# A kernel for attention and two mixtures of experts: the sum and the sending of an expert's second tile stand behind the branch over its third tile

## The chip, the cores and the metric

One core of one Trainium2 chip. The metric is the time of one execution on the device in microseconds (us), and of several runs the median.

## The reference

Three layers follow one another on 4608 tokens of 512 numbers, in float32:

```python
attn = exp(scale * q_c @ k_c^T - max) / (sum + 1e-9); x = attn @ v_c   # in chunks of 64, 8 heads
# _moe_ref
do_compute = x @ w_skip > 0
logits = xc @ w_gate; e_idx = argmax(logits); gate_w = softmax(logits)[e_idx]
for e in range(8):                          # each token that is computed goes to one expert
    h = maximum(xc[mask] @ w1[e], 0)        # 512 -> 1024
    y[mask] = gate_w[mask, None] * (h @ w2[e])
out = x.copy(); out[do_compute] = xc + y    # the other tokens stay as they are
# _moe2_ref
h = maximum(maximum(x @ w1, x @ w2), x @ w3)
return h @ w_out
```

How many tokens an expert gets is known only when the kernel runs.

## The kernel before, in words

The core does the attention (up to some 175 us), the middle layer of eight experts (some 190 to 480 us) and the last layer (to the end). Every number is held as a high and a low part, so a product of two matrices is three products on TensorE (PE): `mm3`, lines 663 to 665.

**Tokens.** The attention leaves its rows in `x_dram`. For each expert the rows of its tokens are gathered in tiles of 128 by indirect DMAs of GpSimd (POOL) (`gather`, L554 to L564), through a list of slots. A tile's result is added to its rows by VectorE (DVE) and sent back by an indirect DMA of POOL (`put_back`, L940 to L949: the sum is L941, the send L943). Two buffers of four tiles hold rows; expert e uses buffer e mod 2, named `xg_4030` for experts 2, 4 and 6 and `xg_4126` for 1, 3, 5 and 7 in what follows. So tile j of expert e + 2 may be gathered only when tile j of expert e has been sent; `gather_tiles` says so by a dependency on that send. Sends and gathers go out in POOL's program order, and each waits for the one that used its semaphore (`DMASW0` to `DMASW7`, in turn) before it.

**One expert.** For experts 1 to 6 `first_tiles` computes the first two tiles together:

- `h`: 96 products of 256 columns, which ScalarE (ACT) and DVE evacuate as `hhi` and `hlo`;
- `ahead`: the next expert's tiles 2 and 3 are gathered, and the rows of this expert's third tile are turned (`trm`, L584, transposes on PE; ACT and DVE evacuate them as `xhi` and `xlo`, L587 and L588);
- `y_0`: the first tile's 24 products and its `put_back`; `amid`, which is `turn_next`, turns the next expert's first two tiles, `trm_0` and `trm_1`;
- `y_1`: the second tile's 24 products and its `put_back`.

Behind that stands the branch `tc.If(n_e[e] > 2 * P)` (L1240): the third tile (`single`) and, inside it, a branch for the fourth (`beyond`, L1189) and for more (L1193, L1194). With this input experts 2, 3 and 5 take the branch, 2 and 3 with a fourth tile; experts 1, 4 and 6 jump over it. Expert 7 begins with one tile alone (`main`), then two more.

**Weights.** An expert has eight pieces of weights. SyncE loads each, ACT makes its high part (`whi`, L93) and DVE its low part (`wlo`, L94). The next expert's pieces 0, 1, 2, 3 and 7 (`EARLY`) are written in front of `first_tiles`, and 6, 4 and 5 (`LATE`) behind the branch. Products of `y` go by `KF_ORDER`, so they use the pieces 7, 6, 4 and 5, six products each.

**Order.** A scheduler sets the order on each engine within a straight stretch of the program, by dependencies and by its own costs. What is bound to a branch can't leave its side of it. Eight banks of PSUM hold accumulators: five "mm", two "tr" for transposes and one "t3"; before the change transposes rotate over all three of `t3, tr, tr`, and `y` over "mm".

Of the kernel before, what the change touches and what calls it, by code (L numbers as in the profile page):

```python
# [40 lines left out]
def kernel(  # L41
# [15 lines left out]
    nc = tc.nc  # L57
# [12 lines left out]
    def ps(tag, name):  # L70
        pool, bufs = banks[tag]
        return pool.tile([P, 512], F32, tag=tag, name=name, bufs=bufs)
# [4 lines left out]
    def take_turns(**tags):  # L77
        for use, among in tags.items():
            turns[use] = cycle(among)

    def ps_mm(name):
        return ps(next(turns["mm"]), name)
# [466 lines left out]
    def apart(ins, own, other):  # L549
        for grp in (own, other):  # L550
            tc.declare_no_dep(ins.ins, group=grp, reason="tiles of tokens share no row")
        tc.add_to_no_dep_group(own, ins.ins)
# [98 lines left out]
    vm, big, big_T, units, xt, groups, slots, picks, xgs, xT, link, put, sent = {}, {}, {}, {}, {}, {}, {}, {}, {}, {}, {}, {}, ([], [])  # L651
# [286 lines left out]


    def put_back(key, xg, ids, acc):  # L940
        nc.vector.scalar_tensor_tensor(  # L941
            xg[:, :DM], acc, xg[:, DM:DM + 1], xg[:, :DM], op0=ALU.mult, op1=ALU.add)
        ins = nc.gpsimd.indirect_dma_start(  # L943
            out=x_dram[:, :], out_offset=bass.IndirectOffsetOnAxis(ap=ids, axis=0),
            in_=xg, in_offset=None,
            bounds_check=N - 1, oob_is_err=False,
        )
        apart(ins, "put", "get")
        put.setdefault(key, []).append(ins.ins.name)  # L949

    def relu_split(hi, lo, src):
        return (
            nc.scalar.activation(hi, src, AF.Relu),
            nc.vector.scalar_tensor_tensor(lo, src, 0.0, hi.bitcast(F32), op0=ALU.max, op1=ALU.subtract),
        )

    def second_acc(name, key, hhi, hlo, i, xg, tag=None):
        n = xg.shape[0]
        acc = (ps(tag, f"y_{name}") if tag else ps_mm(f"y_{name}"))[:n]
        sl = slice(i * P, i * P + n)  # L960
        for n, kf in enumerate(KF_ORDER):
            bhi, blo = ew[key[0], 4 + kf // 2]
            mm3(acc, hhi[:, kf, sl], hlo[:, kf, sl], bhi[:, kf % 2, :], blo[:, kf % 2, :], n == 0, n == 7)
        return acc

    def second(name, key, hhi, hlo, i, xg, ids):
        put_back(key, xg, ids, second_acc(name, key, hhi, hlo, i, xg))

    def first_tiles(name, e, xT, xgs, idss, between, side=(), amid=None):
        hi, lo = xT  # L970
        w = hi.shape[2]
        hhi = bpool.tile([P, 8, w], F32R, tag="b8", name=f"hhi_{name}")
        hlo = bpool.tile([P, 8, w], F32R, tag="b8", name=f"hlo_{name}")
        per = 512 // w
        for n in range(0, 8, per):
            f0 = KF_ORDER[n]
            acc = ps_mm(f"h_{name}_{n}")[:, :per * w].rearrange("p (f t) -> p f t", f=per)
            for j in range(per):
                f = f0 + j
                for c in range(KC):  # L980
                    ahi, alo = ew[e, c]
                    link["main"] = mm3(acc[:, j, :], ahi[:, f * P:(f + 1) * P], alo[:, f * P:(f + 1) * P],
                        hi[:, c, :], lo[:, c, :], c == 0, c == KC - 1)
            done = relu_split(hhi[:, f0:f0 + per, :], hlo[:, f0:f0 + per, :], acc)
            if n % 2 == 2 - per and side:
                with tc.issue_after(done[0].ins), tc.issue_after(done[1].ins):
                    side.pop(0)()
        between()
        for i in range(2):
            second(f"{name}_{i}", (e, i), hhi, hlo, i, xgs[i], idss[i])  # L990
            if i == 0 and amid:
                amid()
        return hhi, hlo

    def single_rows(name):
        return [four_kb([P, 8, P], F32R, f"h{nm}_{name}", True) for nm in ("hi", "lo")]
# [31 lines left out]

    def idc(e, j):
        return ids_0[:, j:j + 1] if e == 0 and j < 3 else ids_sb[:, e * COLS + j:e * COLS + j + 1]  # L1030

    def tiles_of(rows):
        return [rows[:, j, :] for j in range(4)]
# [153 lines left out]
    def beyond(e, t3):  # L1187
        xg = xgs[e][3]
        with tc.If(n_e[e] > 3 * P):  # L1189
            if t3 is None:  # L1190
                t3 = rows_T(f"{e}_3", [xg])
            single(f"{e}_3", (e, 3), t3, xg, idc(e, 3))
            with tc.If(n_e[e] > 4 * P):  # L1193
                with tc.For_i(4, nt_e[e], 1) as j:  # L1194
                    ids = mpool.tile([P, 1], I32, tag="ids", name=f"ids_{e}")
                    nc.vector.tensor_copy(ids, ids_sb[:, bass.ds(j + e * COLS, 1)])
                    gather(xg, ids, alone=True)
                    single(f"{e}_n", (e, 3), rows_T(f"{e}_n", [xg], t3), xg, ids)

    for e in range(E):  # L1200
        def ahead():
            if e + 1 < E:
                gather_tiles(e + 1, [2, 3])
            turn_ahead()

        def turn_ahead():
            xT[e, 2] = rows_T(f"{e}_2", xgs[e][2:3])

        def turn_next():
            if e + 2 < E:  # L1210
                xT[e + 1] = rows_T(f"{e + 1}", xgs[e + 1][:2])
            else:
                xT[e + 1] = rows_T(f"{E - 1}_0", xgs[e + 1][:1])

        if 0 < e < E - 1:
            gather_tiles(e + 1, [0, 1])
        free = [wpool] * ((WA - 2 * held) // 2) + [wpool2] * ((WB - 2 * (E - held)) // 2)
        early_a = len([p for p in free if p is wpool])
        if 0 < e < E - 1:
            for i in EARLY:  # L1220
                expert_piece(e + 1, i, free.pop(0))
        side = [lambda i=i: sums_ahead(i) for i in range(sum(STEPS[:e]), sum(STEPS[:e + 1]))]
        later, side = (side, []) if e == 0 else ([], side)
        if 0 < e < E - 1:
            first_tiles(f"{e}", e, xT[e], xgs[e], [idc(e, 0), idc(e, 1)], ahead, side, turn_next)
        raws = {i: load_raw(*expert_src(e + 1, i)) for i in LATE} if e + 1 < E else {}
        if e == 0:
            n_e, nt_e = [
                [nc.values_load(cnt_i[0:1, c:c + 1], min_val=0, max_val=m) for c in range(c0, c0 + E)]
                for c0, m in ((0, N), (E, COLS))]  # L1230
            n_seam = nc.values_load(cnt_i[0:1, 2 * E:], min_val=0, max_val=N)
        third = (xT[e, 2], xgs[e][2], idc(e, 2)) if e < E - 1 else None
        with ExitStack() as pinned:
            if e == 0:
                for ins in link["rows"]:
                    pinned.enter_context(tc.issue_after(ins.ins))
                for chunk in later:
                    chunk()
            elif e + 1 < E:
                with tc.If(n_e[e] > 2 * P):  # L1240
                    t3 = single(f"{e}_2", (e, 2), *third, lambda: rows_T(f"{e}_3", xgs[e][3:]))
                    beyond(e, t3)
            else:
                main = single(
                    f"{e}_0", (e, 0), xT[e], xgs[e][0], idc(e, 0), lambda: rows_T(f"{e}", xgs[e][1:3]))
                with tc.If(n_seam > 3 * P):
                    for j in (1, 2):
                        single(f"{e}_{j}x", (e, j), rows_T(f"{e}_{j}x", [xgs[e][j]]), xgs[e][j], idc(e, j))
                    beyond(e, None)
                    for j in (1, 2):  # L1250
                        nc.gpsimd.memset(idc(e, j), N)
                load_first()
                sums_room(0, 0)

                def turn_first():
                    with tc.issue_after(link["main"].ins):
                        sums_T(0, 0)

                first_tiles(f"{e}", e, main, xgs[e][1:3], [idc(e, 1), idc(e, 2)], turn_first, side)
                ring_ahead(0, 0, 5)  # L1260
                sums_room(0, 1)
                sums_T(0, 1)
            for n, i in enumerate(LATE if e + 1 < E else []):
                pool = wpool if n < held else wpool2
                early_a += pool is wpool
                expert_piece(e + 1, i, pool, None, raws[i])
        if e == 0:
            beyond(0, None)
        held = early_a
# [65 lines left out]
    for b, (r0, n) in enumerate(BLOCKS):  # L1335
# [31 lines left out]
        for half in range(2):  # L1367
            for i in range(n // P):
                acc = ps_mm(f"o_{b}_{half}_{i}")
# [45 lines left out]
```

## Time and profile before

| | us |
|---|---|
| median of three runs | 1044.71 |
| the three runs | 1044.71, 1053.66, 1044.31 |
| the profiled execution | 1041.12 |
| its span (first to last instruction) | 1039.4 |

The trace is of that one profiled execution; its times count from the start of the span. Each engine has its own row of instructions, so the time that an engine waits in front of an instruction, and what ended that wait, stand in brackets behind the row. A releaser is inferred: where an instruction waits for several things, the one is named that came last by the record, which may not be the one that held it. The record of an indirect DMA on POOL is the instruction; when its data has arrived is told in a row of its own.

### The profile page before, as it was taken

What the parts mean: (1) busy time and instruction counts of PE and PEld (TensorE: products, weight loads), DVE (VectorE), ACT (ScalarE), POOL (GpSimd) and SP (SyncE); (2) the same over time, 40 slices, a digit from 0 to 9 for tenths busy, and PEclk for the clock granted to TensorE, in tenths of its full rate; (3) what the DMA queues carried; (4) which work ended last, traced back from release to release, by engine and by line L of the source; (5) the groups of instructions that cost most, each with busy time, mean ns of one, the idle gap of its engine ahead of it and who ended that gap; (6) DMA issues with size and microseconds to landing.
All of it is one profiled execution on the core that took longest, in us unless ns stands there. A gap on an engine that the chain in (4) does not pass through costs nothing.

```text
span 1039.4 us, 19677 instructions
## 1 busy us (share of the span) xinstructions
PE 993.9 (96%) x7569; PEld 850.8 (82%) x7569; DVE 572.1 (55%) x1100; ACT 420.1 (40%) x762; POOL 316.6 (30%) x359
## 2 busy tenths in 40 slices
PE   7989899998999999899999999999999999999996
PEld 6988898887787898687878888788788888878995
DVE  4667798687282895555897524343334424434241
ACT  5877674455252554333443422223222322223230
POOL 3666857512140432105331502223012312103010
PEclk8999999999999999899999999999999999999999
DMA  9999973777272896569994456645566356674771
GB/s 235 289 313 301 232 238 111 248 271 259 91 252 94 295 322 221 176 206 353 332 325 151 152 152 177 200 120 172 162 196 188 104 168 200 187 224 153 228 229 40
DMA packets 198258, 217.44 MB, mean 209 GB/s; under 512 B 47195, under 2 KB 162027, under 8 KB 198144
## 3 DMA queue, kind: packets, MB, share of 16 engines
q1 hardware_dynamic: 185328, 176.27, 56.0%
q0 software_dynamic: 10224, 31.40, 8.7%
q10 hardware_dynamic: 2592, 8.26, 2.1%
q8 instruction: 70, 1.15, 0.5%
q14 instruction: 44, 0.36, 0.1%
HBM read 175.30 MB, written 41.98 MB: 209 GB/s over the span
## 4 chain that ended last, share of the span: by engine, by line
PE 51%; DMA 5%; DVE 2%; issue 1%; SPq 0%; ACT 0%; DVEq 0%; ACTq 0%; POOLq 0%
PE f_a L663 6%; PE f_a L665 6%; PE f_a L664 6%; PE o L663 5%; PE o L665 5%; PE o L664 5%; PE f_d L663 3%; DMA ws<-m_sums 3%; PE f_d L665 3%; PE f_d L664 3%; PE f_b L663 2%; PE f_b L665 1%; PE f_b L664 1%; PE trf L1126 1%; DMA x<-x_dram 1%; PE h L663 1%
## 5 line engine op out<-in xcount | busy, mean ns | idle before, releaser
L94 POOL TENSOR_TENSOR fh<-best,fh 128x512 fp32r<-128x512 f32 (+1 forms) x60 | 75.2, 1258 | 358.1 <-ACT fh L93 272.7
L663 PE MATMUL f_a<-x_t,ws 128*128 128x512 f32 (+1 forms) x270 | 100.1, 372 | 0.8 <-DVE best L1298 0.8
L665 PE MATMUL f_a<-x_t,ws 128*128 128x512 f32 (+1 forms) x270 | 99.4, 368 | 0.0
L664 PE MATMUL f_a<-x_t,ws 128*128 128x512 f32 (+1 forms) x270 | 99.4, 368 | 0.0
L664 PE MATMUL o<-wlo_m,fh 128*128 128x512 f32 x216 | 84.5, 391 | 0.0
L663 PE MATMUL o<-whi_m,fh 128*128 128x512 f32 x216 | 84.4, 391 | 0.0
L665 PE MATMUL o<-whi_m,fh 128*128 128x512 f32 x216 | 83.3, 393 | 0.0
L93 ACT CAST whi_e<-raw_e 128x1024 fp32r<-128x1024 f32 x56 | 57.8, 1050 | 58.3 <-DMA raw_e<-in_moe_w_dram 30.1
L663 PE MATMUL h<-xhi,whi_e 128*128 128x256 f32 x256 | 73.4, 287 | 7.7 <-PEq L1240 3.5
L94 DVE TENSOR_TENSOR wlo_e<-raw_e,whi_e 128x1024 fp32r<-128x1024 f32 x56 | 67.6, 1222 | 22.9 <-ACT whi_e L93 21.7
L943 POOL DMA_INDIRECT x_dram<-xg,ids_sb x20 | 25.1, 1257 | 169.5 <-DVE xg L941 81.9
L663 PE MATMUL y<-whi_e,hhi 128*128 128x512 f32 x184 | 73.8, 402 | 0.9 <-ACT hhi L1014 0.9
L93 ACT CAST fh<-best 128x512 fp32r<-128x512 f32 (+1 forms) x60 | 34.5, 579 | 94.5 <-DVE best L1300 57.5
L664 PE MATMUL h<-xlo,whi_e 128*128 128x256 f32 x256 | 72.5, 283 | 0.0
L665 PE MATMUL y<-whi_e,hlo 128*128 128x512 f32 x184 | 72.2, 396 | 0.2
L665 PE MATMUL h<-xhi,wlo_e 128*128 128x256 f32 x256 | 72.4, 283 | 0.0
L664 PE MATMUL y<-wlo_e,hhi 128*128 128x512 f32 x184 | 71.7, 391 | 0.0
L1132 POOL TENSOR_TENSOR x_t<-t,x_t 128x512 fp32r<-128x512 f32 (+1 forms) x40 | 46.1, 1183 | 51.0 <-ACT x_t L1131 50.9
L1303 ACT COPY p<-f_a 128x512 f32<-128x512 f32 (+1 forms) x45 | 24.3, 543 | 86.5 <-PE f_a L665 86.3
L663 PEld LDWEIGHTS f_a<-x_t,ws 128*128 128x128 f32 x270 | 50.9, 189 | 9.9 <-DVE best L1298 1.6
L665 PEld LDWEIGHTS f_a<-x_t,ws 128*128 128x128 f32 x270 | 50.9, 189 | 8.6
L664 PEld LDWEIGHTS f_a<-x_t,ws 128*128 128x128 f32 x270 | 50.9, 189 | 8.2
(242 smaller groups left out, 2599.7 us busy)
## 6 DMA issues: line engine op xcount, KB each, us to landing
ws<-m_sums SPq DMA_DIRECT2D x135, 512.0 KB
raw_e<-in_moe_w_dram SPq DMA_DIRECT2D x64, 512.0 KB
ws<-m_sums SPq DMA_DIRECT2D x45, 256.0 KB
x_dram<-xg POOLq DMA_DIRECT2D x9, 1040.0 KB, 6.5
x<-x_dram SPq DMA_DIRECT2D x36, 256.0 KB
v_all<-in_v_dram SPq DMA_DIRECT2D x32, 256.0 KB
out_dram<-os SPq DMA_DIRECT2D x32, 256.0 KB
m_sums<-n_raw ACTq DMA_DIRECT2D x18, 448.0 KB
```

The source lines that it names most:

```text
L93: nc.scalar.copy(hi, src),
L94: eng.tensor_tensor(lo, src, hi.bitcast(F32), op=ALU.subtract),
L663: nc.tensor.matmul(acc, ahi, bhi, start=first, stop=False, skip_group_check=onto)
L664: nc.tensor.matmul(acc, ahi, blo, start=False, stop=False, skip_group_check=onto)
L665: return nc.tensor.matmul(acc, alo, bhi, start=False, stop=last, skip_group_check=onto)
L943: ins = nc.gpsimd.indirect_dma_start(out=x_dram[:, :], out_offset=bass.IndirectOffsetOnAxis(ap=ids, axis=0), in_=xg, in_offset=None, bound ...
L1126: nc.tensor.transpose(tr[:, i * P:(i + 1) * P], row[:, c * P:(c + 1) * P], ident)
L1132: eng.tensor_tensor(lo, src, hi.bitcast(F32), op=ALU.subtract)
L1303: nc.scalar.copy(p1, acc_a)
```

## The change

The second tile's products get the bank `t3`, to which no transposes go inside the two tiles' block any more (they rotate over two banks of "tr"), and the rotation is set back behind the branch. `first_tiles` no longer calls `put_back` for the second tile but returns a function that does; it is called behind the branch, and `behind` binds both its instructions, the sum and the send, to the end of the branch. They are bound by an order alone, without a semaphore. The change is in the loop over experts 1 to 6.

```diff
     def put_back(key, xg, ids, acc):
-        nc.vector.scalar_tensor_tensor(
+        added = nc.vector.scalar_tensor_tensor(
             xg[:, :DM], acc, xg[:, DM:DM + 1], xg[:, :DM], op0=ALU.mult, op1=ALU.add)
...
         put.setdefault(key, []).append(ins.ins.name)
+        return added, ins
...
         between()
-        for i in range(2):
-            second(f"{name}_{i}", (e, i), hhi, hlo, i, xgs[i], idss[i])
-            if i == 0 and amid:
-                amid()
-        return hhi, hlo
+        second(f"{name}_0", (e, 0), hhi, hlo, 0, xgs[0], idss[0])
+        if not amid:
+            second(f"{name}_1", (e, 1), hhi, hlo, 1, xgs[1], idss[1])
+            return None
+        amid()
+        take_turns(tr=["tr"])
+        acc = second_acc(f"{name}_1", (e, 1), hhi, hlo, 1, xgs[1], "t3")
+        return lambda: put_back((e, 1), xgs[1], idss[1], acc)
...
+    def behind(block, *got):
+        for ins in got:
+            tc.add_manual_dep(
+                ins.ins, block.name,
+                mybir.DependencyInfo(mybir.DependencyClass.NoSync, mybir.DependencyReason.DATA),
+                reason="behind the branch")
...
-            first_tiles(f"{e}", e, xT[e], xgs[e], [idc(e, 0), idc(e, 1)], ahead, side, turn_next)
+            put_last = first_tiles(f"{e}", e, xT[e], xgs[e], [idc(e, 0), idc(e, 1)], ahead, side, turn_next)
...
                     t3 = single(f"{e}_2", (e, 2), *third, lambda: rows_T(f"{e}_3", xgs[e][3:]))
                     beyond(e, t3)
+                behind(nc.cur_bb.bb.instructions[-1], *put_last())
+                take_turns(tr=["t3", "tr", "tr"])
```

**POOL at the end of expert 2's branch.** Rows with `x_dram<-xg` are sends, rows with `xg<-x_dram` gathers of expert 4's rows. Before, the first row is the third tile's send; behind the branch come the second tile's send and the gathers of expert 4's tiles 1, 2 and 3.

```order
L943 DMA x_dram<-xg_4030,ids_sb 4609x520 [waits DMASW0_49,DVE_49]
L1240 UNCONDITIONAL_BRANCH
L1240 ISA [waits DMASW6_49,DMASW7_49,DMASW5_49,DMASW0_49]
L1240 UNCONDITIONAL_BRANCH
L943 DMA x_dram<-xg_4030,ids_sb 4609x520 [waits DMASW5_49,DVE_49]
L555 DMA xg_4030<-x_dram,ids_sb 128x520 [waits DMASW6_49]
L555 DMA xg_4030<-x_dram,ids_sb 128x520 [waits DMASW7_49,DVE_49,PE_49]
L555 DMA xg_4030<-x_dram,ids_sb 128x520 [waits DMASW0_49,DVE_49,PE_49]
```

In the change the first row is again the third tile's send; behind the branch stand the first tile's send, the gathers of expert 4's tiles 0, 2 and 3, the second tile's send and the gather of expert 4's tile 1.

```order
L943 DMA x_dram<-xg_4030,ids_sb 4609x520 [waits DMASW6_49,DVE_49]
L1251 UNCONDITIONAL_BRANCH
L1251 ISA [waits DMASW5_49,DMASW6_49,DMASW4_49,DMASW3_49]
L1251 UNCONDITIONAL_BRANCH
L943 DMA x_dram<-xg_4030,ids_sb 4609x520 [waits DMASW3_49,DVE_49]
L555 DMA xg_4030<-x_dram,ids_sb 128x520 [waits DMASW4_49]
L555 DMA xg_4030<-x_dram,ids_sb 128x520 [waits DMASW5_49,DVE_49,PE_49]
L555 DMA xg_4030<-x_dram,ids_sb 128x520 [waits DMASW6_49,DVE_49,PE_49]
L943 DMA x_dram<-xg_4030,ids_sb 4609x520 [waits DMASW7_49,DVE_49]
L555 DMA xg_4030<-x_dram,ids_sb 128x520 [waits DMASW0_49]
```

The first tile's send has slid behind the branch too, and the gather of tile 1 from the front of three gathers to their end, behind the second tile's send. In both, the gather of tile 3 waits for the semaphore that the third tile's send used (`DMASW0` before, `DMASW6` now). Behind expert 3's branch the second tile's send moves behind the gathers of expert 5's tiles 2 and 3 in the same way; the first tile's doesn't move, and there it is the gather of tile 1 that waits for the semaphore of the third tile's send.

**PE in expert 3, near the end of the first tile's products.** `trm_1_6033` are the transposes of expert 4's tile 1, `y_0` and `y_1` the two tiles' products. Before:

```order
L664 MATMUL y_0_5995<-wlo_e_5_5799,hhi_5838 128x512
L584 MATMUL trm_1_6033<-ident,xg_4030 128x128 [waits DMASW6_49,PE_49]
L584 MATMUL trm_1_6033<-ident,xg_4030 128x128 x2
L665 MATMUL y_0_5995<-whi_e_5_5798,hlo_5839 128x512 [waits DVE_49]
L663 MATMUL y_0_5995<-whi_e_5_5798,hhi_5838 128x512
L664 MATMUL y_0_5995<-wlo_e_5_5799,hhi_5838 128x512
L665 MATMUL y_0_5995<-whi_e_5_5798,hlo_5839 128x512
L584 MATMUL trm_1_6033<-ident,xg_4030 128x128
L663 MATMUL y_1_6040<-whi_e_7_5288,hhi_5838 128x512 [waits PE_49]
```

In the change:

```order
L664 MATMUL y_0_5995<-wlo_e_5_5799,hhi_5838 128x512
L584 MATMUL trm_1_6033<-ident,xg_4030 128x128 [waits DMASW0_49]
L584 MATMUL trm_1_6033<-ident,xg_4030 128x128 x3
L665 MATMUL y_0_5995<-whi_e_5_5798,hlo_5839 128x512 [waits DVE_49]
L663 MATMUL y_0_5995<-whi_e_5_5798,hhi_5838 128x512
L664 MATMUL y_0_5995<-wlo_e_5_5799,hhi_5838 128x512
L665 MATMUL y_0_5995<-whi_e_5_5798,hlo_5839 128x512
L663 MATMUL y_1_6040<-whi_e_7_5288,hhi_5838 128x512 [waits DVE_49]
```

The four transposes stand together and wait for the gather that is now the last of POOL's (`DMASW0`), and `y_1` waits for DVE, the last reader of its bank.

**DVE from expert 6 to expert 7.** `wlo_e_6`, `wlo_e_4` and `wlo_e_5` are the low parts of expert 7's late pieces, `hlo` and `xlo` those of its first tile's hidden rows and of its next rows. Before:

```order
L94 TENSOR_TENSOR wlo_e_6_7952<-raw_e_6_7684,whi_e_6_7951 128x1024 [waits DMAHW4_49,PE_49,Activation_49]
L94 TENSOR_TENSOR wlo_e_4_7956<-raw_e_4_7686,whi_e_4_7955 128x1024 [waits DMAHW6_49,Activation_49]
L94 TENSOR_TENSOR wlo_e_5_7960<-raw_e_5_7688,whi_e_5_7959 128x1024 [waits DMAHW7_49,Activation_49]
L588 TENSOR_TENSOR xlo_8010<-trm_0_8011,xhi_8009 128x4x128 [waits Activation_49]
L1015 TENSOR_TENSOR hlo_0_7964<-trh_0_1_7995,hhi_0_7963 128x512 [waits Activation_49]
L1015 TENSOR_TENSOR hlo_0_7964<-trh_0_0_8002,hhi_0_7963 128x512 [waits Activation_49]
L588 TENSOR_TENSOR xlo_8010<-trm_1_8018,xhi_8009 128x4x128 [waits Activation_49]
```

In the change:

```order
L94 TENSOR_TENSOR wlo_e_2_7461<-raw_e_2_7458,whi_e_2_7460 128x1024 [waits DMAHW7_49,Activation_49]
L941 SCALAR_TENSOR_TENSOR xg_4030<-y_1_7655,xg_4030 128x512 [waits DMASW4_49,PE_49]
L94 TENSOR_TENSOR wlo_e_3_7467<-raw_e_3_7464,whi_e_3_7466 128x1024 [waits DMAHW1_49,Activation_49]
L94 TENSOR_TENSOR wlo_e_7_7473<-raw_e_7_7470,whi_e_7_7472 128x1024 [waits DMAHW3_49,Activation_49]
L1019 TENSOR_TENSOR hlo_0_7964<-trh_0_1_7995,hhi_0_7963 128x512 [waits Activation_49]
L1019 TENSOR_TENSOR hlo_0_7964<-trh_0_0_8002,hhi_0_7963 128x512 [waits Activation_49]
L94 TENSOR_TENSOR wlo_e_6_7952<-raw_e_6_7680,whi_e_6_7951 128x1024 [waits DMAHW5_49,Activation_49]
L588 TENSOR_TENSOR xlo_8010<-trm_0_8011,xhi_8009 128x4x128 [waits Activation_49]
L588 TENSOR_TENSOR xlo_8010<-trm_1_8018,xhi_8009 128x4x128 [waits Activation_49]
L94 TENSOR_TENSOR wlo_e_4_7956<-raw_e_4_7682,whi_e_4_7955 128x1024 [waits DMAHW6_49,Activation_49]
L94 TENSOR_TENSOR wlo_e_5_7960<-raw_e_5_7684,whi_e_5_7959 128x1024 [waits DMAHW7_49,Activation_49]
```

The splits of the pieces 2, 3 and 7 and the second tile's sum of expert 6 have come behind expert 6's branch, and the splits of 6, 4 and 5 behind the two `hlo`.

## Rows read from the trace of the kernel before

**Rows 1.** The page's head: span, and busy time, share and instructions by engine.

```profile
span 1039.4 us, 19677 instructions
...
PE 993.9 (96%) x7569; PEld 850.8 (82%) x7569; DVE 572.1 (55%) x1100; ACT 420.1 (40%) x762; POOL 316.6 (30%) x359
```

**Rows 2.** PE's waits: who ended them, us in total, times, the longest.

```profile
PE h L663 <- PEq L1240: 7.0, 3, 3.5
...
PE h L663 <- DVE xg L941: 0.9, 1, 0.9
...
PE y L663 <- ACT hhi L1014: 0.9, 3, 0.3
```

**Rows 3.** POOL's timeline behind expert 2's branch: start, us, instruction, idle before.

```profile
291.91 1.78 POOL L943 DMA_INDIRECT x_dram<-xg,ids_sb  x1 [1.69 <-DVE wlo_e L94]
...
300.30 1.38 POOL L555 DMA_INDIRECT xg<-x_dram,ids_sb  x1 [2.44 <-DVE n_q L641]
308.49 1.20 POOL L943 DMA_INDIRECT x_dram<-xg,ids_sb  x1 [6.81 <-DVE xg L941]
310.00 1.84 POOL L555 DMA_INDIRECT xg<-x_dram,ids_sb  x1 [0.30 <-issue]
```

**Rows 4.** The gathers of line 555: start to landing of their data.

```profile
L555 POOL DMA_INDIRECT xg<-x_dram,ids_sb x29: 992/1206/2446, 196.3 to 409.1; - x29
...
DMA to landing us min/median/max: 4.8/6.7/7.9
```

**Rows 5.** The DMA view of 305 to 315: issues, median us to landing.

```profile
xg<-x_dram,ids_sb POOLq DMA_INDIRECT x1, 7.4
```

**Rows 6.** PE's timeline in expert 3, around the transposes of expert 4's rows.

```profile
305.08 0.60 PE L584 MATMUL trm<-ident,xg 128*128 128x128 f32 x4
...
305.98 0.49 PE L584 MATMUL trm<-ident,xg 128*128 128x128 f32 x3
```

**Rows 7.** POOL's timeline behind expert 3's branch.

```profile
342.29 1.72 POOL L943 DMA_INDIRECT x_dram<-xg,ids_sb  x1 [1.88 <-DMA x_dram<-xg,ids_sb]
...
350.63 0.99 POOL L555 DMA_INDIRECT xg<-x_dram,ids_sb  x1 [2.22 <-DVE n_q L640]
```

**Rows 8.** PE's timeline in expert 4, the last transpose of expert 5's tile 1.

```profile
357.53 0.27 PE L584 MATMUL trm<-ident,xg 128*128 128x128 f32 x1
```

**Rows 9.** DVE's timeline in expert 1.

```profile
227.94 2.35 DVE L94 TENSOR_TENSOR wlo_e<-raw_e,whi_e 128x1024 fp32r<-128x1024 f32 x2
230.21 0.68 DVE L588 TENSOR_TENSOR xlo<-trm,xhi 128x512 fp32r<-128x512 f32 x1
```

**Rows 10.** PE's timeline in expert 1, its two tiles' products mixed.

```profile
229.14 0.39 PE L663 MATMUL y<-whi_e,hhi 128*128 128x512 f32 x1
229.37 0.39 PE L664 MATMUL y<-wlo_e,hhi 128*128 128x512 f32 x1
```

**Rows 11.** PE's timeline at the start of expert 7.

```profile
436.97 0.60 PE L584 MATMUL trm<-ident,xg 128*128 128x128 f32 x4
437.41 0.60 PE L1012 MATMUL trh<-ident,h_1s 128*128 128x128 f32 x4
437.89 0.66 PE L1012 MATMUL trh<-ident,h_0s 128*128 128x128 f32 x4
438.85 0.50 PE L663 MATMUL y<-whi_e,hhi 128*128 128x512 f32 x1 [0.31 <-ACT hhi L1014]
```

**Rows 12.** ACT's timeline at the start of expert 7.

```profile
437.23 0.60 ACT L1006 ACTIVATE h_0s<-h 128x512 f32<-128x512 f32 x1 [0.67 <-PE h L665]
...
438.19 1.10 ACT L1014 CAST hhi<-trh 128x512 fp32r<-128x512 f32 x2
```

**Rows 13.** DVE's timeline in expert 6: a split of a piece, an `hlo`.

```profile
404.35 1.22 DVE L94 TENSOR_TENSOR wlo_e<-raw_e,whi_e 128x1024 fp32r<-128x1024 f32 x1
405.48 0.68 DVE L954 SCALAR_TENSOR_TENSOR hlo<-h,hhi 128x512 fp32r<-128x512 f32 x1
```

**Rows 14.** PE's timeline: the first product behind the branches of experts 1 and 6.

```profile
238.19 0.35 PE L663 MATMUL h<-xhi,whi_e 128*128 128x256 f32 x1 [3.22 <-PEq L1240]
...
428.53 0.76 PE L663 MATMUL h<-whi_e,xhi 128*128 128x512 f32 x1 [3.53 <-PEq L1240]
```

**Rows 15.** The view by stretches behind them: us, busy times, granted clock (PEclk), DMA share, GB/s.

```profile
238.20:245.20 7.00, 7.00 (x58) 7.00 (x59) 5.37 (x6) 4.45 (x6) 5.16 (x4) 1.00 0.73 234
428.50:435.30 6.80, 6.77 (x17) 5.35 (x18) 1.23 (x1) 2.12 (x3) 0.00 (x0) 0.54 0.24 92
```

## The prediction

> **What bounds the kernel now.** The page's line of busy times comes first [rows 1]: TensorE (PE) works for 993.9 of 1039.4 us, 96%; VectorE (DVE) has 55%, GpSimd (POOL) 30%. So an edit counts only by what it adds to, or takes from, the 45 us in which PE stands. The table of PE's waits [rows 2] says who ends them. The sum that is moved here, `put_back`, makes PE wait once, for 0.9 us; the evacuation of a third tile's hidden rows (`y` behind `hhi`) costs 0.9 in three waits; the branch itself (`PEq L1240`) 7.0 in three. So the reader is to see that there is little to win: the sum of the second tile delays no product, and its place matters only to the queues that it shares. Of those, POOL's timeline is the third view [rows 3], since POOL gives out every send and gather of token rows in one order, and PE's next transposes wait for the gathers. The profiled execution took 1041.12 us (1039.4 of span and 1.7 around it); the runs' median is 1044.71, 3.6 above it. I make the sum against the first and add it to the second.
>
> **The change, part by part.** Its arithmetic is the same: 24 products, one sum and one send, in each of experts 1 to 6. What moves is order.
>
> *POOL behind expert 2's branch.* Before, POOL sends tile 3, tile 2 (at 291.91 [rows 3]), tile 1, and then gathers expert 4's tiles 1, 2 and 3; the last gather starts at 300.30, 8.39 us after tile 2's send. The order shows why: it waits for the semaphore that this send used. In the change the tile-0 send and gather take the front places, tiles 2 and 3 follow, that same wait stands at the gather of tile 3, and the send of tile 1 comes behind it, and only then the gather of expert 4's tile 1. So: 300.30 + 1.38 for the gather in front, 0.30 between two of them, a send of 1.0 (1.20 at 308.49), 0.30 again: it starts at 303.3. Its row on POOL is no arrival. Arrival is counted from the start in the row on landing [rows 4], 4.8 to 7.9 us with a median of 6.7; the one gather that stands straight behind a send on a busy queue, as this will, is that at 310.00, and took 7.4 [rows 5]. I take 7.4, which gives 310.7. PE wants the rows for the second transposes inside expert 3's first tile, at 305.98 [rows 6]. Behind them in PE's order is all the rest of that tile, so PE stands: **+4.7** (2.1 to 5.2 by the ends of the landing row). Tile 0's gather, now at 295.3, would land at 302.7, in time for the first transposes at 305.08.
>
> [...]
>
> *POOL behind expert 3's branch.* Here tile 0's send isn't moved. The wait for tile 2's send (350.63, 8.34 after 342.29 [rows 7]) falls on the gather of expert 5's tile 1 itself: at 350.63 + 7.4 it lands at 358.0. PE's need: before, the last of these transposes is at 357.53 [rows 8], and the change puts all four in front of the last four products (0.91) and three of the transposes behind the first (0.33): 356.3. **+1.7** (0 to 2.2).
>
> *Expert 1's second tile.* Its accumulator takes the bank `t3`. In experts 2 to 6 that bank's last user is the third tile's transposes, long read. In expert 1 it is the first transposes of expert 2's rows, and DVE finishes their low half at 230.21 + 0.68 = 230.9 [rows 9], behind two weight splits. Before, the two tiles' products were mixed; now y_1 comes behind y_0, whose last product would start at 229.14, so y_1 could 0.23 later, at 229.4 [rows 10]. **+1.5** (0, if DVE comes earlier, to 1.6).
>
> *The seam from expert 6 to 7.* With the sum behind the branch, DVE's splits of the pieces 6, 4 and 5 stand behind the hidden rows of expert 7's first tile, whose two halves now end together on PE. Before, `y` began 1.88 us behind the last `h` (436.97 to 438.85 [rows 11]). Now two evacuations of 0.60, transposes of 0.48 and a cast of 0.55 [rows 11, 12] follow one another: 2.2, or +0.3. DVE then has the second `hlo` (0.68), split 6 (1.22), two `xlo`, split 4 (1.22) [rows 13], done 4.1 and 6.7 us behind the last `h`. The eighth product wants split 6 at 2.2 + 7 x 0.23 = 3.8, the fourteenth split 4 at 5.9 (with the 0.3 and 0.4 of transposes). **+1.4** (0 to 2.5, both splits uncovered).
>
> *Inside the taken branches* (experts 2, 3, 5) the transposes of the fourth tile now stand behind two products of the third, which can fill the three waits of 0.3 [rows 2]: **-0.5** (-0.9 to +0.5).
>
> *From expert 5 to 6* two splits of expert 6's pieces move behind the branch on DVE. PE takes three accumulators in turn there and reaches them only by the 17th product. **0** (to one split, 1.2).
>
> *Experts 4 and 6, where the branch is skipped:* nothing stands between, so the move costs nothing there; the cover is the empty body.
>
> Sum: 4.7 + 1.7 + 1.5 + 1.4 - 0.5 + 0 = **+8.8**, so 1049.9 beside the profiled 1041.1, and 1053.5 against the median.
>
> **The rivals.**
>
> *A, slower: the waits also cost the clock.* PE's two longest stands around a branch are 3.22 us at 238.19 and 3.53 at 428.53 [rows 14]. [...] The wait of 4.7 in expert 3 is longer than both. For A: length, and that PE has nothing else in that order. [...] It decides from 1.6 us of lost clock on.
>
> *B, the waits are hidden.* If the gather lands like the quickest, 4.8, expert 3 waits 2.1 and expert 4 not at all; with the seam and expert 1 covered too the sum is 1.6 to 3, so 1046 to 1048. The case that the change does nothing at all belongs here: its wait takes the place of other waits downstream, 1044 to 1046. For it: expert 4's load is close to its need. Against: 4.8 is the quickest of 29 gathers, and half of them took over 6.7.
>
> [...]
>
> **How the numbers follow.** Chances: forecast 0.40, A 0.32, B 0.19, C 0.09. The forecast is 1053.5; its own range, not all ends together, 1050 to 1056. The range of 1043.5 to 1060 takes in B, A with one or two falls, and C with the waits; it leaves out C alone and A with the bounds added. A measurement here can't tell less than about 1% (10.4 us) from no change. Slower by more is above 1055.2: A, and the top of the forecast, 0.34. Faster by more is below 1034.3: the far end of C, 0.03. Within: 0.63.
>
> **What would show it.** PE idle of 4 to 5 us near 306 in front of the transposes from expert 4's rows, ended by a gather, with POOL's gather started some 3 us later than the last one of before; 1 to 2 us at the same place of expert 4; a wait for `xlo` of about 1.5 in expert 1; two waits for splits behind expert 7's first `y`. A granted clock below 1.00 behind 306 shows A. If the gather is on time, or tile 1's gather goes out ahead of tile 3's, the largest term is wrong; if the branch's gaps shrink below 1 us, C is right.

## The result, and the profile after

The change makes the kernel **slower: 1.0094 times the time before, 95% interval 1.0067 to 1.0121** (medians of 13 runs each, 1057.70 against 1048.93 us). The ratio comes to 9.9 us, 0.94% (7.0 to 12.7 us by its interval); the medians are 8.8 us apart, 0.84%. Predicted was +8.8 us, 0.84%. As a time, 1053.5 was forecast, and 4.2 less than was measured, since the median of before rose from the 1044.71 of three runs to the 1048.93 of these 13.

The profiled execution of the change took 1065.58 us, the longest of its 13. Of its 24.5 us above the profiled one of before, 12.7 lie ahead of expert 1, where both programs are the same: up to there the clock's falls cost 15.4 us in this trace and 5.1 in that of before. So I compare from the first product of expert 1 to the first of the last layer, the stage that holds the change: 210.92 to 471.99 before, 223.60 to 499.12 after. The view by stretches of before (us; busy times of PE, PEld, DVE, ACT, POOL; granted clock; DMA share; GB/s):

```profile
210.92:471.99 261.07, 248.77 (x1461) 215.92 (x1461) 167.88 (x249) 114.12 (x159) 60.83 (x45) 0.99 0.65 222
```

and of after, the whole stage and its four stretches at a granted clock of 0.50:

```profile
223.60:499.12 275.52, 255.66 (x1460) 219.58 (x1461) 166.93 (x250) 113.58 (x159) 56.89 (x45) 0.97 0.62 211
...
244.93:248.34 3.41, 3.41 (x10) 2.63 (x9) 2.48 (x3) 0.76 (x2) 0.94 (x1) 0.50 0.80 274
255.17:258.58 3.41, 3.41 (x18) 3.41 (x18) 3.07 (x4) 2.20 (x3) 1.36 (x2) 0.50 0.51 131
326.85:330.26 3.41, 3.41 (x11) 2.67 (x10) 2.25 (x5) 1.64 (x2) 0.48 (x1) 0.50 0.97 316
470.21:477.04 6.83, 6.16 (x29) 6.19 (x30) 0.03 (x1) 0.66 (x2) 0.00 (x0) 0.50 0.69 206
```

The stage is 14.45 longer. PE stands 19.86 us in it (275.52 - 255.66) against 12.30: +7.56. It is busy 6.89 more, of which I put 5.1 down to the granted clock: half of 17.06 us at 0.50, 8.53, against 3.41 before (half of 6.83 at 0.50). 1.8 is left, 1.4 of it in expert 6's products, and has no cause that I could show. In the first experiment below, a program with the same order on every engine, the same stage is 10.2 longer with no more clock lost than before. That is near the difference of the runs, so I lay the change's account by the waits, and look at the clock apart. PE's waits (who ended them, us in total, times, longest), after:

```profile
PE h L663 <- PEq L1259: 3.8, 1, 3.8
...
PE h L663 <- PEq L1251: 3.2, 2, 2.9
PE trm L584 <- DMA xg<-x_dram,ids_sb: 2.6, 1, 2.6
PE trh L1016 <- ACT h_1s L1010: 2.2, 1, 2.2
PE y L663 <- DVE xlo L588: 2.1, 1, 2.1
...
PE y L664 <- DVE wlo_e L94: 1.1, 3, 0.7
```

and in the first experiment, `no_binding`:

```profile
PE trm L584 <- DMA xg<-x_dram,ids_sb: 4.7, 2, 2.9
PE h L663 <- PEq L1259: 3.5, 1, 3.5
PE h L663 <- PEq L1252: 3.0, 3, 1.5
...
PE trh L1016 <- ACT h_1s L1010: 2.4, 1, 2.4
PE y L663 <- DVE xlo L588: 1.5, 1, 1.5
...
PE y L664 <- DVE wlo_e L94: 0.9, 2, 0.7
```

Against [rows 2], the gather, the hidden rows (`h_1s`), the low half `xlo` and the splits are new. The branches of experts 1 to 6 (L1251 after, L1240 before) cost less, 3.2 instead of 7.0. The branch inside expert 7 (L1259) costs 3.8. Before, PE stood 0.94 at this place, the row `h` behind `DVE xg L941` of [rows 2], and that was the sum's. The last product in front ends near 445.4, the sum follows, and the first product of the next tile comes 0.15 behind the sum's end (DVE's row, then PE's):

```profile
445.40 0.75 DVE L941 SCALAR_TENSOR_TENSOR xg<-y,xg 128x512 f32<-128x512 f32 x1 [3.71 <-PE y L665]
...
446.30 0.36 PE L663 MATMUL h<-xhi,whi_e 128*128 128x256 f32 x1 [0.94 <-DVE xg L941]
```

PE's branch instruction ran beside it from 442.3, for 3.5 us, and so was over at 445.85, ahead of the sum.

**The gather.** POOL behind expert 2's branch, after:

```profile
309.50 1.55 POOL L943 DMA_INDIRECT x_dram<-xg,ids_sb  x1 [1.65 <-DVE xg L941]
311.35 1.94 POOL L943 DMA_INDIRECT x_dram<-xg,ids_sb  x1 [0.30 <-DVE wlo_e L94]
313.60 1.05 POOL L555 DMA_INDIRECT xg<-x_dram,ids_sb  x1 [0.30 <-issue]
314.96 1.82 POOL L555 DMA_INDIRECT xg<-x_dram,ids_sb  x1 [0.31 <-issue]
317.08 1.47 POOL L555 DMA_INDIRECT xg<-x_dram,ids_sb  x1 [0.30 <-DVE hlo L955]
318.85 1.02 POOL L943 DMA_INDIRECT x_dram<-xg,ids_sb  x1 [0.30 <-DVE n_q L600]
320.18 1.03 POOL L555 DMA_INDIRECT xg<-x_dram,ids_sb  x1 [0.30 <-issue]
```

The order is the predicted one: the gather of tile 3 at 317.08, behind it tile 1's send, and only then, at 320.18, the gather that PE wants first. The wait that was predicted in it isn't there. Before, POOL stood idle for 2.44 us ahead of its last gather [rows 3]; here it stands 0.30 ahead of the gather at 317.08, as ahead of every other from 311.35 on, and the 7.58 us from tile 2's send to it are POOL's own work on the sends and gathers between. `no_binding` has the same 0.30. PE's timeline has its end:

```profile
326.34 0.66 PE L584 MATMUL trm<-ident,xg 128*128 128x128 f32 x4 [2.57 <-DMA xg<-x_dram,ids_sb]
```

**The seam.** ACT's timeline at the start of expert 7, which answers to [rows 12]:

```profile
456.32 1.04 ACT L93 CAST whi_e<-raw_e 128x1024 fp32r<-128x1024 f32 x1 [3.78 <-DMA raw_e<-in_moe_w_dram]
457.27 0.59 ACT L1010 ACTIVATE h_1s<-h 128x512 f32<-128x512 f32 x1
457.76 0.59 ACT L1010 ACTIVATE h_0s<-h 128x512 f32<-128x512 f32 x1
```

and PE's, which answers to [rows 11], from the hidden rows to the first product behind the branch:

```profile
457.91 0.65 PE L1016 MATMUL trh<-ident,h_1s 128*128 128x128 f32 x4 [2.18 <-ACT h_1s L1010]
...
461.98 0.50 PE L664 MATMUL y<-wlo_e,hhi 128*128 128x512 f32 x1 [0.15 <-DVE wlo_e L94]
...
464.31 0.49 PE L664 MATMUL y<-wlo_e,hhi 128*128 128x512 f32 x1 [0.67 <-DVE wlo_e L94]
...
470.88 0.55 PE L663 MATMUL h<-xhi,whi_e 128*128 128x256 f32 x1 [3.77 <-PEq L1259]
```

ACT stood 3.78 us for the load of a weight piece, and the hidden rows came behind that cast. The load is late since its raw buffer came free late. DVE's split frees a buffer, and SyncE's load into it goes out right behind:

```profile
448.12 1.22 DVE L94 TENSOR_TENSOR wlo_e<-raw_e,whi_e 128x1024 fp32r<-128x1024 f32 x1
...
449.36 0.38 SPq L100 DMA_DIRECT2D raw_e<-in_moe_w_dram  x1
```

Before, the load of the same piece went out at 416.49, 15.1 us behind expert 6's first product (401.40); here it is 25.1 us (424.23). The split at 448.12 stands in front of expert 6's branch in both orders, so the three splits of expert 7 that have come behind that branch (450.08, 452.56 and 457.39) aren't what held this load. The trace leads further back: three splits of expert 6's own pieces now stand behind expert 5's branch (424.49 and 427.37), and with three buffers for raw pieces a later load waits for an earlier split. This chain is read from the trace; no run changes it alone. Then PE met late splits, three waits of 1.1 us together, and stood 3.77 at the branch, where before it stood 0.94.

### The profile page after: what moved, and what is told of

Its sections match the earlier page's. It is cut to its first block, busy times and chain, and to the rows that moved or that the text cites. A ratio compares the mean times of both kernels' runs of the same rounds, so it can differ in the third digit from the quotient of the medians.

```text
span 1063.9 us, 19661 instructions
## 1 busy us (share of the span) xinstructions
PE 1012.1 (95%) x7569; PEld 864.2 (81%) x7569; DVE 569.9 (54%) x1100; ACT 419.1 (39%) x762; POOL 312.4 (29%) x359
## 4 chain that ended last, share of the span: by engine, by line
PE 48%; DMA 4%; DVE 2%; issue 1%; SPq 0%; ACT 0%; POOL 0%; POOLq 0%; ACTq 0%; DVEq 0%
PE f_a L663 6%; PE f_a L665 6%; PE f_a L664 6%; PE o L663 5%; PE o L664 5%; PE o L665 5%; PE f_d L663 3%; PE f_d L665 3%; PE f_d L664 3%; DMA ws<-m_sums 2%; PE f_b L663 2%; PE f_b L665 2%; PE f_b L664 2%; PE trf L1137 1%; DMA x<-x_dram 1%
## 5 line engine op out<-in xcount | busy, mean ns | idle before, releaser
L663 PE MATMUL h<-xhi,whi_e 128*128 128x256 f32 x256 | 75.7, 297 | 10.3 <-PEq L1259 3.8
L665 PE MATMUL y<-whi_e,hlo 128*128 128x512 f32 x184 | 74.5, 406 | 0.1
L663 PEld LDWEIGHTS h<-xhi,whi_e 128*128 128x128 f32 x256 | 51.7, 202 | 12.9 <-issue 11.8
```

Source lines behind the costliest of these rows:

```text
L663: nc.tensor.matmul(acc, ahi, bhi, start=first, stop=False, skip_group_check=onto)
L665: return nc.tensor.matmul(acc, alo, bhi, start=False, stop=last, skip_group_check=onto)
```

## The experiments

Ratios are to the kernel before on the same chip, with 95% intervals. "Stage" is the stage above, less that of before, in the profiled executions; the clock lost in it is given where it isn't the 3.41 of before.

**no_binding: the bank without the binding.** (The binding without the bank wasn't tried: the five banks of the other accumulators go round inside the branch.)

```diff
+            put_last()                       # behind first_tiles, ahead of the branch
...
-                behind(nc.cur_bb.bb.instructions[-1], *put_last())
```

> The binding is left out: the second tile's sum and send are called in front of the branch, and only the bank is changed. The order on every engine comes out as in the change, because the scheduler puts both behind the branch by itself once the second tile's products stand behind the first's. Theory 1 (the waits of the change: expert 1's bank 2.1 us, the gather in expert 3 2.6, the seam to expert 7 about 2, and the clock behind them): 1.009 of before, as the change, with the same three waits. Rival (the binding itself costs): 1.000 to 1.003.

1.0085 [1.0052, 1.0118]; stage +10.2. The binding does nothing of its own: the scheduler puts the sum behind the branch even when it is left free. The cost comes with the bank and the order that follows from it.

**put_first and put_first_23: the sum and the send in front of the branch**, in all six experts and in experts 2 and 3.

```diff
-                with tc.If(n_e[e] > 2 * P):
+                with ExitStack() as late:
+                    for ins in put_last():
+                        late.enter_context(tc.issue_after(ins.ins))
+                    late.enter_context(tc.If(n_e[e] > 2 * P))
```

> The bank is kept, but the branch is issued behind the second tile's sum and send in all six experts, as before the change. Theory 1: no wait for a gather in expert 3, the splits for expert 7 on time again, expert 1's wait for its bank of about 2 us stays: 2 to 4 us over before, 1.002 to 1.004. Rival 2 (the bank and the unmixed products cost, the move costs nothing): 1.009.

> As the change, but in experts 2 and 3 the sum and the send stand in front of the branch, so that POOL gathers tile 1 of experts 4 and 5 first of the three. Theory 1: the wait of 2.6 us in expert 3 goes, and the fall of the clock behind it (1.7): 4 us less than the change, 1.005 of before. Rival 2: as the change, 1.009.

1.0161 [1.0126, 1.0195], and 1.0114 [1.0067, 1.0161]; clock lost 6.83 in both. PE's wait for the gather went, as expected, and the total got worse, which no theory had. The waits of `put_first`:

```profile
PE h L663 <- PEq L1251: 9.0, 3, 4.7
...
PE trm L584 <- DVE xg L941: 5.8, 5, 2.5
```

With the sum early, its bank `t3` is free early, and a transpose of the next expert's third tile, which takes that bank next, moves in front of the branch, and there PE waits for the sum, 5.8 us in five times. So the cost turns on who follows in that bank, which the next two try.

**bank_turn: the transposes' banks start their turn anew before expert 1.**

```diff
         if e == 0:
             beyond(0, None)
+            take_turns(tr=["t3", "tr", "tr"])
```

> As the change, but the turn of the transposes' banks is set back once more in front of expert 1, so that its third tile has the bank t3 and not expert 2's first. Theory 1: expert 1's wait of 2.1 us goes, and a fall of the clock behind it (1.7 or two): 2 to 5 us less than the change, 1.004 to 1.007 of before; the gather in expert 3 still makes PE wait 1 to 3 us. Rival 2 (mixing lost, not the bank): 1.009.

1.0042 [1.0011, 1.0072]; stage +9.3 with 6.83 of clock lost, so +5.9 without. The wait for `xlo` in expert 1 is gone, but PE stands 4.98 at expert 1's branch behind it, where the change stands 2.14 for `xlo` and 2.86 at the branch: 5.00. So this trace shows no time won at that place; that the turn costs time rests on the ratio, which is below the change's by little more than the intervals. Gathers still end 3.7 us of waits, and the branch in expert 7 costs 3.1.

**own_bank: `t3` for the second tile's products alone**, the transposes take turns on two banks.

```diff
-                take_turns(tr=["t3", "tr", "tr"])
+                if e == E - 2:
+                    take_turns(tr=["t3", "tr", "tr"])
...
+            take_turns(tr=["tr"])            # once, before expert 1
```

> As the change, but the bank t3 serves the second tile's products alone in experts 1 to 6, and all transposes turn over two banks; sum and send stay behind the branch. Then y_1 need not wait for transposes in expert 1, and the next expert's second transposes move back behind y_1's first products, so their gather has more time. Theory 1: no wait in expert 1, none or under 1 us for a gather in experts 3 and 4, the seam to expert 7 as in the change (about 2.4 for the hidden rows, 0.7 for a split): 5 to 7 us less than the change, 1.002 to 1.005 of before. Rival 3 (two banks for transposes are too few, or the move itself costs): 1.008 or more.

1.0031 [1.0004, 1.0059]; stage +6.9 with 6.83 lost, +3.5 without. No wait for gathers, `xlo` or late hidden rows is left; beside a split's 0.6, the branch in expert 7 stays (its expectation has the late hidden rows stay too, and that of `own_bank_6` builds on them):

```profile
451.53 0.36 PE L663 MATMUL h<-xhi,whi_e 128*128 128x256 f32 x1 [3.52 <-PEq L1260]
```

So about 0.6 of the change's 0.94% were the price of sharing the bank.

**own_bank_first: and the branch ordered behind the sum and the send.**

```diff
+    def ahead_of(block, *got):               # order only: no wait
+        for ins in got:
+            tc.add_manual_dep(
+                block, ins.ins.name,
+                mybir.DependencyInfo(mybir.DependencyClass.NoSync, mybir.DependencyReason.DATA),
+                reason="ahead of the branch")
...
+            last = put_last()
...
-                behind(nc.cur_bb.bb.instructions[-1], *put_last())
+                ahead_of(nc.cur_bb.bb.instructions[-1], *last)
```

> As own_bank, but the branch stands behind the sum and the send in the order of DVE and POOL, so nothing is moved behind it. Theory 1: as own_bank, and at the seam the casts of pieces 3 and 7 stand in front of the branch again, so y of expert 7 begins as in before: 0.999 to 1.002. A rival on the sum itself (in front of the branch it delays PE): 1.004 or more, with waits of PE for L941 or for a cast at the branches that are skipped.

**0.9975 [0.9946, 1.0005]**; stage -0.2. The same product as above waits as it did before:

```profile
445.36 0.36 PE L663 MATMUL h<-xhi,whi_e 128*128 128x256 f32 x1 [0.94 <-DVE xg L941]
```

With a bank that nobody shares and the sum in front, nothing of the change's cost is left, and nothing measurable is won over the kernel before.

**own_bank_6, own_bank_146, own_bank_26: the sum in front in some experts only** (own_bank_first's `ahead_of` in the experts named, for 26 in 2 to 6; `behind` in the others).

> As own_bank, but in expert 6 alone sum and send stand in front of the branch; of the casts of expert 7's pieces only that of piece 7 is left in front of its hidden rows on ACT. Theory 1 (ACT's cast waits for a load and holds up the hidden rows): the wait of 2.4 at the seam falls below 1, 1 to 3 us less than own_bank. Rival (the seam's wait is the two evacuations one behind the other): 2.0 to 2.4 stay, as own_bank.

> As own_bank, but sum and send stand behind the branch only in the experts that take it (2, 3 and 5) and in front of it in 1, 4 and 6. Theory 1: the seam to expert 7 is that of before, as in own_bank_first, and the three waits of 0.3 inside the taken branches are filled: 0.995 to 1.001 of before, 0 to 3 us less than own_bank_first. Rival (the move behind a taken branch costs): 1.002 or more.

> As own_bank_first, but in expert 1 sum and send stay behind the branch. Theory 1: between own_bank_first and own_bank_146, 0.995 to 1.001 of before; the stand at the branch of expert 1 is 2 to 4 us as before. Rival (the sum in front of the branches is what costs in put_first): 1.004 or more.

1.005 [1.0023, 1.0077], 1.0066 [1.0037, 1.0094] (clock lost 8.53) and 0.9984 [0.9954, 1.0013] (1.71). The first two missed. With expert 6's sum in front alone, expert 6's own branch costs 4.3 and expert 7's 3.46; the splits behind expert 5's branch stay there in both. In `own_bank_146` the split of piece 5 still stands behind both `xlo`, so a split's place depends on the bindings of the earlier experts too:

```profile
447.07 1.28 DVE L588 TENSOR_TENSOR xlo<-trm,xhi 128x512 fp32r<-128x512 f32 x2
448.27 1.22 DVE L94 TENSOR_TENSOR wlo_e<-raw_e,whi_e 128x1024 fp32r<-128x1024 f32 x1
```

PE's branch there begins at 450.8 and PE stands 3.60. In `own_bank_first` and `own_bank_26`, where the last split is over before `xlo`, it stands 0.94.

**gather_first: the change, with the gathers of tiles 2 and 3 ordered behind tile 1's.**

```diff
+            got = gather(xgs[e][j], idc(e, j))
...
+            if j > 1 and ("second", e) in link:
+                behind(link["second", e].ins, got)
```

> As the change, with one more order: the gathers of a next expert's tiles 2 and 3 go out behind that of its tile 1. Theory 1: in expert 3 the gather of tile 1 starts some 3 us earlier than in the change, PE waits 0 to 2 there instead of 2.6 to 2.9, 1 to 4 us less than the change; expert 1's wait and the seam stay: 1.005 to 1.008 of before. Rival 2 (the gather's place does not matter, its landing is late whatever its place): 1.009.

1.0076 [1.0041, 1.0111]; stage +5.7. Expert 3's wait for the gather falls from 2.57 to 1.35; the order alone doesn't take it away. The late hidden rows cost 0.3 here and not the 2.2 that was expected to stay.

**late_once and late_twice: the kernel before, with one split of expert 7 moved behind its two `xlo`**, done once and done twice. Nothing else of the change is in them. Of their times, 1049.79 and 1042.24 us, there is one each, which settles nothing beside the 1035.84 to 1048.87 of the kernel before; they are read by their traces.

```diff
+                    with tc.issue_after(link["rows"][1].ins):
+                        for _ in range(1):   # 2 in late_twice
+                            nc.vector.tensor_tensor(lo, raw, hi.bitcast(F32), op=ALU.subtract)
```

> The kernel before, with one split moved: DVE makes the low part of expert 7's piece 5 behind the two xlo of its rows, and not in front of its hidden rows. It is done about 1 us ahead of its first product, so PE waits for nothing more. Theory 4 (PE's own branch instruction takes 3.3 to 3.9 us in its sequencer and is hidden only as far as the sequencer has run ahead of the products; a product that waits for its operand holds the sequencer): the stand at the branch in front of expert 7's last two tiles grows from 0.94 to 1 to 2 us. Rival (the stand has to do with the binding or with the queues of the change): 0.94 as before.

> As late_once, and the split is made twice over (the same result), so it is done just as its first product's turn comes, some 3.3 us before the last product in front of the branch ends. Theory 4: PE waits under 0.5 us for the split, but the stand at the branch grows to 2.5 to 3.5 us, as in the change. Rival: 0.94 as before.

PE doesn't wait for the split in either by 0.3 us or more, and the stand at expert 7's branch grows from 0.94 to 2.93 and 3.43. The first is more than the 1 to 2 that was expected; the rival's 0.94 is excluded in both. The rows of that branch in PE's sequencer tell why (min/median/max ns, first and last start): of before,

```profile
L1246 PEldq COMPARE_BRANCH  x1: 3507/3507/3507, 442.3 to 442.3; - x1
```

of the change,

```profile
L1259 PEldq COMPARE_BRANCH  x1: 3912/3912/3912, 466.7 to 466.7; - x1
```

of `late_once`,

```profile
L1253 PEldq COMPARE_BRANCH  x1: 3892/3892/3892, 450.0 to 450.0; - x1
```

and of `late_twice`.

```profile
L1253 PEldq COMPARE_BRANCH  x1: 3332/3332/3332, 443.2 to 443.2; - x1
```

The instruction takes 3.3 to 3.9 us in nine traces, of before too: in these four, in `no_binding` (3.57), `own_bank` (3.69), `own_bank_146` (3.43), `own_bank_first` and `own_bank_26` (3.33 each). What differs is how early it begins. DVE's splits in `late_once`:

```profile
447.49 1.21 DVE L1249 TENSOR_TENSOR wlo_late<-raw_e,whi_late 128x1024 fp32r<-128x1024 f32 x1
```

and in `late_twice`:

```profile
439.43 2.48 DVE L1249 TENSOR_TENSOR wlo_late<-raw_e,whi_late 128x1024 fp32r<-128x1024 f32 x2
```

The splits end at 448.70 and 441.91, and the branch begins 1.3 us behind, at 450.0 and 443.2. `no_binding` (453.33 to 454.6), `own_bank` (446.25 to 447.5) and `own_bank_146` (449.49 to 450.8) have the same 1.3. Before, the last split ended at 438.01, long before the branch's 442.3. In the change the last two splits end at 465.39, and the branch begins at 466.7, again 1.3 behind.

```profile
463.04 2.35 DVE L94 TENSOR_TENSOR wlo_e<-raw_e,whi_e 128x1024 fp32r<-128x1024 f32 x2
```

So before, the sequencer was ahead of the products: it took the branch at 442.3, and they ran on to 445.36. That hid 3.0 of its 3.5 us under the products, and the sum in front of the next product covered the rest. In the traces with the 1.3 us a product that needed a late split kept the sequencer back, as I read them; in `late_once` and `late_twice` it did so though the split came in time for the product itself. In `late_twice` the weights of the first such product go in just behind the split:

```profile
441.96 0.19 PEld L664 LDWEIGHTS y<-wlo_late,hhi 128*128 128x128 f32 x1 [0.33 <-DVE wlo_late L1249]
```

The nine traces divide by this. In the six with a late last split (the change, `no_binding`, `own_bank`, `own_bank_146`, `late_once`, `late_twice`) the branch begins 1.3 us behind that split's end, and PE stands 2.93 to 3.77 us. In the three with an early one (before, `own_bank_first`, `own_bank_26`) it begins 3.0 us ahead of the end of the last product, and PE stands 0.94, for the sum. That is +2.0 to +2.8 us without a wait that names the split. Of the other five traces the tables of waits give the stand alone: 0.9 for the sum in `put_first`, and 3.0 to 3.5 at the branch in `put_first_23`, `bank_turn`, `gather_first` and `own_bank_6`.

## Why the prediction was right or wrong

The sign and the sum were right, the sum partly by luck: of the parts, two losses at the seam were put too low or left out, and a gain of nearly their size, which the sum had put at nothing, and gathers that cost less than predicted made up for them. Below, each in us of PE's standing; `no_binding` has the same order as the change and shows how much one execution differs from the next:

| step | predicted | change | no_binding |
|---|---|---|---|
| expert 3, gather | +4.7 | +2.57 | +2.9 |
| expert 4, gather | +1.7 | 0 | +1.75 |
| expert 1, bank `t3` | +1.5 | +2.14 | +1.5 |
| seam, hidden rows | +0.3 | +2.18 | +2.4 |
| seam, splits | +1.1 | +1.1 | +0.9 |
| branch in expert 7 | 0 | +2.8 | +2.5 |
| branches of experts 1 to 6 | 0 | -3.5 | -4.0 |
| taken branches | -0.5 | +0.2 | +0.1 |
| sum | +8.8 | +7.5 | +8.0 |

The tables of waits hold these to a tenth; PE's standing in the stage differs by 7.56 and 8.20. Some 2 us of longer busy time come on top in both.

- **The gather** came late by the order that was predicted, but not by the wait. The step "that same wait stands at the gather of tile 3" failed: 8.39 us from tile 2's send were carried over, and POOL needed 7.58 for its work alone, without a wait. So the gather starts 13.6 us behind expert 3's first product and not 14.4; and its rows land 6.1 us after its start, not 7.4. I had taken one row [rows 5] over the median of 29 [rows 4]; the median, 6.7, was nearer. The distinction between the instruction's end and the landing held: it ends at 321.21, PE's transposes start at 326.34.
- **Expert 4** lies on its edge: no wait in one execution, 1.75 in the other, inside the 0 to 2.2.
- **Expert 1's bank** was right as a wait: 2.14 and 1.5 for `xlo`, and with the bank's turn set anew in `bank_turn` the wait is gone. What it costs in time is less clear, since the stand at the branch behind it grew there by as much.
- **The seam** failed in the step "a cast of 0.55 ... follow one another: 2.2, or +0.3". I followed only the work of the hidden rows and DVE's queue behind them. A split that moves later also frees its raw buffer later, the load that wants the buffer starts later (25.1 us behind expert 6's first product and not 15.1), and ACT's cast of that load stood in front of the evacuation: 2.2 to 2.4 us. By the trace this begins at the step "From expert 5 to 6 ... **0**", which asked only when PE reaches the splits and not which loads wait for them. That link is argued. For it: `own_bank_6` and `own_bank_146`, with expert 6's sum in front again and expert 5's behind, keep the long stand at expert 7's branch (3.46 and 3.60); `own_bank_26`, with both in front, has 0.94. The wait of the hidden rows isn't fixed, either: with the same sums behind the branches, `own_bank` and `gather_first` have 0.3 of it and `bank_turn` 0.3, with 1.6 at the `hhi` behind it; `own_bank` stands 3.65 at expert 6's branch instead.
- **The branch in expert 7** had no term at all. The 0.9 of [rows 2] was a wait for the sum, as I read it; but beside it ran a branch of 3.5 us, hidden under products, which no row of the table of waits shows. In `late_once` and `late_twice` a late split uncovers it: +2.0 and +2.5 there, +2.8 in the change.
- **Rival C**, that the gaps at the branches go, happened in part. The branch stand of expert 6 fell from 3.53 [rows 14] to 0.34, by my own sign below 1 us. The gain of 3.5 and 4.0 us over all these branches, and gathers cheaper by 3.8 and 1.7 than predicted, stand against the two losses at the seam that I missed (4.7 and 4.6), which is why the sum came out. Whether the change made it isn't shown. `late_once` and `late_twice` have the order of before up to expert 6's branch, and stand 2.81 and 1.13 there; the branch instruction of expert 6 took 6.63 us before and 3.45 in the change. Over the variants these stands run from 0.34 to 4.98.
- **Rival A**: the two long stands of before [rows 14] already spoke both ways, since a fall came behind one of them alone [rows 15]. My range counts a fall as 3.1 us, 6.80 x 0.46 by [rows 15], in A's 1060 and in C; no run shows one of that size behind expert 3's wait. What follows it in the change and in `no_binding` is 3.41 us at 0.50, 1.7 us lost. And before's own fall behind expert 6's branch, 3.4 us lost by 6.83 at 0.50, is missing in both. The trace of the change has a net loss of 5.1, that of `no_binding` none, and their ratios agree within their intervals. Over all runs the mean granted clock is 0.981 in the change and 0.986 in `no_binding`, against 0.984 of before beside it. So A isn't needed for the result.
- **Rival B** failed: the waits were there.

The words "bound behind the branch" misled me as to the cause: the order comes with the bank. What costs is that the transposes share the bank (about 0.6%, by the change against `own_bank`) and that work of DVE stands behind the branches (the rest, by `own_bank` against `own_bank_first`).

## What to carry to other kernels

When work moves later on one engine, follow the buffer that it frees, through all later loads and not only the next: each load that waits for it, and what stands behind that load's consumer on the next engine. A branch can be far longer than it looks: here it took 3.3 to 3.9 us in nine traces, and PE stood 0.94 where the sequencer took it 3.0 us ahead of the last product's end, but 2.93 to 3.77 where an operand came late for a product shortly before it, and the wait showed under the branch's name. In a profile that doesn't show the branch among the waits, it may be there all the same, as the 3.5 us of before were. A bank that is given to a new user takes over the order of those who share it: give it to that user alone, or set the turn anew.

## What the runs showed of the hardware

In the trace of before PE's compare-and-branch took from 0.07 to 6.6 us. Nine of one line (L1240) (min/median/max ns):

```profile
L1240 PEldq COMPARE_BRANCH  x9: 71/184/6631, 231.6 to 421.6; - x9
```

The median of these nine is 184 ns. Those of experts 1 and 6 took 6.3 and 6.6 us in this trace, and expert 7's (L1246) 3.5. These three skip a body, but so does expert 4's, which took 0.33, and no run here shows what makes one long. In the change expert 6's took 3.45 us instead of 6.63.
